# Loading the weights of the last two chunks in halves, to move the last store to another semaphore

## Chip, cores, metric

One core of a Trainium2 chip. PE is TensorE (matrix products), ACT is ScalarE, DVE is VectorE and POOL is GpSimd. The metric is the device time of one execution in microseconds (us). It lies 1.8 us above the span of the profile.

## The reference

```python
B, S, D, F = 32, 32, 1024, 3584          # all bf16
def reference(x, w_gate, w_up, w_down):
    return (gelu_tanh(x @ w_gate) * (x @ w_up)) @ w_down
```

1024 tokens, two matrices of 1024 x 3584 and one of 3584 x 1024. The kernel spends fewer multiplications than that by working with sums and differences of quadrants of the matrices; those sums are made on POOL (GpSimd) and wait for weights.

## The kernel before

The first stage goes through 14 chunks of weights; the second multiplies by `w_down`. Weights of a chunk are loaded two chunks ahead, by SyncE:

```python
    def load_w(eng, ci, which, d0, d1):
        f0 = ci * FC * P
        src = (wg_r, wu_r)[which]
        eng.dma_start(out=w_tiles[ci, which][:, d0:d1, :], in_=src[:, d0:d1, f0 : f0 + FC * P])

    def load_w_all(ci, which):
        alloc_w(ci, which)
        load_w(nc.sync, ci, which, 0, KD if which == 0 and is_ahead(ci) else DT)
```

At the end four tiles are cast from PSUM and stored, the last one by ACT:

```python
        for m in range(MT):
            r0 = NB + m * P
            o = late.tile([P, NB], bf16, name="o_sb", tag="o_sb", bufs=MT)
            (nc.vector.tensor_copy if m % 2 == 0 else nc.scalar.copy)(o, banka[m])
            nc.scalar.dma_start(out=of[r0 : r0 + P, :NB], in_=o)
```

The framework adds the semaphores (counters that one part of the chip raises and another waits for). In the built program DMAs take eight semaphores in turn, in program order; a DMA raises its semaphore by 16 as its parts land (the trace of the kernel before has 1472 such steps for 92 DMAs). At the end SyncE waits for all of them, two semaphores to a wait: first 3 and 2, then 4 and 1, then 5 and 0, then 6 and DVE's, then 7 and ACT's. Before the change the last store is on DMA semaphore 3, so the *first* of the five waits is the one that really waits.

## Time and profile before

275.1 us, median of three runs (274.97 to 275.95). The profiled run took 274.77 us.

The page of the kernel before (share of the span behind each engine; then the chain of work that ended last, as shares of the span):

```profile
span 273.0 us, 3360 instructions
## 1 busy us (share of the span) xinstructions
PE 268.6 (98%) x1206; PEld 188.7 (69%) x1206; DVE 195.3 (72%) x196; ACT 110.9 (41%) x181; POOL 108.1 (40%) x55
...
## 4 chain that ended last, share of the span: by engine, by line
PE 98%; ACT 0%; DVE 0%; issue 0%
```

PE is the limit from start to end. A change that is to gain anything must shorten PE's work or one of the two ends of the span, where PE is not busy all the time (27.56 of the first 28.50 us, and not at all after 269.51, the end of its last matmul). The windows of the kernel before (PE's busy time is the second number) show no idle PE in the middle:

```profile
core 0: us, PE busy (x) PEld busy (x) DVE busy (x) ACT busy (x) POOL busy (x), PEclk, DMA share, GB/s
0.00:28.50 28.50, 27.56 (x134) 13.17 (x134) 15.15 (x18) 9.75 (x12) 0.70 (x6) 1.00 0.85 212
...
100.00:180.00 80.00, 80.00 (x358) 56.86 (x357) 51.15 (x67) 42.76 (x78) 48.26 (x22) 1.00 0.29 83
180.00:260.00 80.00, 80.00 (x359) 57.23 (x358) 73.13 (x49) 19.39 (x20) 0.00 (x0) 1.00 0.56 181
```

The end, from the timeline of the kernel before (start, duration, engine, line, operation; in brackets what ended the idle time): the last cast, then the issue of the last store.

```profile
269.55 0.58 ACT L580 CAST o_sb<-psA 128x512 bf16<-128x512 f32 x1 [2.59 <-PE psA L440]
270.17 0.34 ACTq L581 DMA_DIRECT2D out_dram<-o_sb  x1
```

What follows is shown by the waits of the DMA queue's engine, SyncE (waiter, releaser, us in total, times, longest): one wait of 23.4 us for stores, and no second one.

```profile
SPq L605 <- DMA out_dram<-o_sb: 23.4, 1, 23.4
```

In the trace itself the last store lands at 271.89 and SyncE's end reads like this (start in us, operation, what it waits for; semaphores by their place among the eight):

```
271.910  wait  DMA 3 and DMA 2      <- the last store is on 3
271.979  wait  DMA 4 and DMA 1
272.041  wait  DMA 5 and DMA 0
272.105  wait  DMA 6 and DVE
272.167  wait  DMA 7 and ACT
272.232  drain, then two barriers of all engines, to 272.984
```

The first wait's record starts 0.02 us after the landing at 271.893, so a record's start is read here as the moment at which the wait is satisfied. The other four, whose last DMA had landed at 268.71, are walked through one by one, 62 to 69 ns from one to the next and 0.257 us from the first to the last. From the landing to the end of the span it is 1.09 us.

POOL's sum that waits for the last weights:

```profile
0.77 2.72 PE L229 MATMUL psA<-const-bfloat16-1.0 128*128 128x512 bf16 x6 [0.77 <-PEq L594]
3.29 0.63 PE L237 MATMUL tp<-ident,x_nat 128*128 128x128 bf16 x4
4.09 0.48 PE L279 MATMUL psC<-b,a12a 128*128 128x256 bf16 x2 [0.17 <-DVE b L240]
...
6.16 0.38 PE L246 MATMUL psA<-b,wg 128*128 128x512 bf16 x1
```

```profile
158.00 2.52 POOL L162 TENSOR_TENSOR s<-wu 128x1024 fp32r<-128x1024 bf16 x1 [4.02 <-DMA wu<-in_w_up_dram]
```

### The profile page before, as it was taken

What the parts mean: (1) busy time and instruction counts of PE and PEld (TensorE: products, weight loads), DVE (VectorE), ACT (ScalarE), POOL (GpSimd) and SP (SyncE); (2) the same over time, 40 slices, a digit from 0 to 9 for tenths busy, and PEclk for the clock granted to TensorE, in tenths of its full rate; (3) what the DMA queues carried; (4) which work ended last, traced back from release to release, by engine and by line L of the source; (5) the groups of instructions that cost most, each with busy time, mean ns of one, the idle gap of its engine ahead of it and who ended that gap; (6) DMA issues with size and microseconds to landing.
All of it is one profiled execution on the core that took longest, in us unless ns stands there. A gap on an engine that the chain in (4) does not pass through costs nothing.

```text
span 273.0 us, 3360 instructions
## 1 busy us (share of the span) xinstructions
PE 268.6 (98%) x1206; PEld 188.7 (69%) x1206; DVE 195.3 (72%) x196; ACT 110.9 (41%) x181; POOL 108.1 (40%) x55
## 2 busy tenths in 40 slices
PE   8999999999999999999999999999999999999994
PEld 4444777877877677676868686754447888888883
DVE  1269996887756676766757656459999999999611
ACT  1271665454543645555463636430300023962001
POOL 1000099997897794948577584000000000000000
PEclk9999999999999999999999999999999999999999
DMA  7994330423504505050513280005992446686202
GB/s 184 292 249 105 95 102 13 118 63 93 156 27 126 151 5 155 0 154 5 151 47 108 67 282 0 0 2 164 346 298 79 129 140 185 218 282 201 78 0 78
DMA packets 53777, 33.77 MB, mean 124 GB/s; under 512 B 9728, under 2 KB 53760, under 8 KB 53760
## 3 DMA queue, kind: packets, MB, share of 16 engines
q1 hardware_dynamic: 50240, 31.00, 39.3%
q10 hardware_dynamic: 3520, 2.56, 2.9%
q8 instruction: 9, 0.15, 0.2%
q14 instruction: 8, 0.07, 0.1%
HBM read 29.62 MB, written 2.10 MB: 116 GB/s over the span
## 4 chain that ended last, share of the span: by engine, by line
PE 98%; ACT 0%; DVE 0%; issue 0%
PE psA L264 34%; PE psA L440 18%; PE psC L264 17%; PE psC L440 7%; PE psB L440 7%; PE psB L264 5%; PE psB L246 3%; PE psA L246 3%; PE psC L279 2%; PE psA L279 1%; PE psA L229 1%; ACT o_sb L580 0%; PE tp L237 0%; DVE b L240 0%
## 5 line engine op out<-in xcount | busy, mean ns | idle before, releaser
L264 PE MATMUL psA<-t,s 128*128 128x512 f32 x208 | 54.1, 402 | 0.0
L256 ACT ACTIVATE h<-c 128x512 bf16<-128x512 f32 x52 | 31.6, 627 | 36.6 <-DVE c L344 36.6
L264 PEld LDWEIGHTS psA<-t,s 128*128 128x128 f32 x208 | 39.1, 188 | 9.2
L162 POOL TENSOR_TENSOR s<-wu 128x1024 fp32r<-128x1024 bf16 x12 | 27.5, 2294 | 24.4 <-PE psC L264 16.0
L344 DVE TENSOR_TENSOR c<-sn,psA 128x512 f32<-128x512 f32 x26 | 17.7, 683 | 16.7 <-PE psA L264 16.7
L264 PEld LDWEIGHTS <-wg 128*128 128x128 bf16 x168 | 15.4, 98 | 20.1 <-issue 3.4
L163 POOL TENSOR_TENSOR s<-s,wg 128x1024 fp32r<-128x1024 f32 x12 | 27.4, 2283 | 0.9
L165 POOL TENSOR_TENSOR s<-wg,wu 128x1024 fp32r<-128x1024 bf16 x12 | 26.6, 2215 | 0.0
L349 ACT COPY sn<-psA 128x512 f32<-128x512 f32 x42 | 23.6, 584 | 6.7 <-PE psA L264 6.7
L349 ACT COPY sn<-psC 128x512 f32<-128x512 f32 x26 | 15.2, 588 | 26.9 <-PE psC L264 22.7
L264 PE MATMUL psA<-t,a22r 128*128 128x512 f32 x104 | 25.9, 391 | 0.0
L264 PE MATMUL psC<-t,s 128*128 128x512 f32 x104 | 25.8, 390 | 0.0
L264 PE MATMUL psC<-b22r,s 128*128 128x512 f32 x104 | 25.7, 389 | 0.0
L264 PE MATMUL psA<-b,wg 128*128 128x512 bf16 x104 | 24.6, 380 | 0.0
L264 PEld LDWEIGHTS psC<-t,s 128*128 128x128 f32 x104 | 19.4, 188 | 4.4 <-ACT ahead L371 0.3
L264 PEld LDWEIGHTS psA<-t,a22r 128*128 128x128 f32 x104 | 19.5, 188 | 4.1
L264 PEld LDWEIGHTS psC<-b22r,s 128*128 128x128 f32 x104 | 19.5, 188 | 4.1
L344 DVE TENSOR_TENSOR c<-sn,psC 128x512 f32<-128x512 f32 x26 | 17.7, 687 | 5.5 <-PE psC L264 5.5
L363 DVE TENSOR_TENSOR hi<-h,psA 128x512 bf16<-128x512 bf16 x14 | 9.6, 688 | 13.9 <-PE psA L264 13.9
L419 DVE TENSOR_TENSOR lo<-c,h 128x512 bf16<-128x512 f32 x12 | 17.9, 1490 | 0.6
L164 POOL TENSOR_TENSOR s<-wg,s 128x1024 fp32r<-128x1024 bf16 x8 | 17.3, 2158 | 0.6
L483 ACT COPY snb<-psC 128x512 f32<-128x512 f32 x4 | 2.2, 590 | 36.5 <-PE psC L440 36.5
(94 smaller groups left out, 413.2 us busy)
## 6 DMA issues: line engine op xcount, KB each, us to landing
wu<-in_w_up_dram SPq DMA_DIRECT2D x13, 512.0 KB, 4.0
wdb<-in_w_down_dram SPq DMA_DIRECT2D x12, 512.0 KB, 5.4
wdb<-in_w_down_dram SPq DMA_DIRECT2D x12, 384.0 KB, 4.8
wg<-in_w_gate_dram SPq DMA_DIRECT2D x8, 512.0 KB, 5.2
v<-in_w_down_dram SPq DMA_DIRECT2D x4, 512.0 KB, 6.4
out_dram<-o_sb ACTq DMA_DIRECT2D x16, 128.0 KB, 1.7
wg<-in_w_gate_dram SPq DMA_DIRECT2D x6, 256.0 KB, 4.5
v<-in_w_down_dram SPq DMA_DIRECT2D x4, 384.0 KB, 8.0
```

Source lines behind the costliest of these rows:

```text
L162: yield eng.tensor_tensor(s1, a21, a22, ADD)
L163: yield eng.tensor_tensor(s2, s1, a11, SUB)
L164: yield eng.tensor_tensor(s4, a12, s2, SUB)
L165: yield eng.tensor_tensor(s3, a11, a21, SUB)
L246: nc.tensor.matmul(ps, lhsT=w_tiles[0, which][:, dt, fl * P : (fl + 1) * P], rhs=x_rows(dt, nb), start=(dt == first), stop=(dt == last),)
L256: nc.scalar.activation(h, src, ACT.Gelu_apprx_tanh)
L264: nc.tensor.matmul(ps, lhsT=lhs[:, k, :], rhs=rhs[:, k, :], start=(start and k == 0), stop=(k == KD - 1), skip_group_check=True,)
L344: tt(t, s, ps, ADD)
L349: nc.scalar.copy(t, ps)
L363: tt(g_of(ft)[:, :NB], h0, psa, MUL)
L419: tt(g_of(ft)[:, NB:], added(sn5[fl], psa[fl]), h1[fl], MUL)
L440: nc.tensor.matmul(banks[m], lhsT=lhs(k)[:, m * P : (m + 1) * P], rhs=rhs(k), start=(start and k == 0), stop=(k == HF - 1), skip_group_che ...
```

## The change

The weights of the last two chunks come in two loads each. That makes four DMAs more, so every later DMA moves on by four of the eight semaphores, and the last store falls on semaphore 7, which the last of the five waits names. The first four waits can then be passed before the last store has landed.

```diff
     def load_w_all(ci, which):
         alloc_w(ci, which)
-        load_w(nc.sync, ci, which, 0, KD if which == 0 and is_ahead(ci) else DT)
+        if ci < NCH - 2:
+            load_w(nc.sync, ci, which, 0, KD if which == 0 and is_ahead(ci) else DT)
+            return
+        for d0 in (0, KD):
+            load_w(nc.sync, ci, which, d0, d0 + KD)
```

## The prediction

> **What bounds the kernel now.** The page gives PE 98% of the span (268.6 of 273.0 us), and the chain that ended last is PE for 98% of it. By windows, PE is busy all 10.00 us of every 10 us from 120 to 260, at granted clock 1.00. DVE (72%), ACT (41%), POOL (40%) and DMA (39% on the main queue) hide behind it. In the timeline the last matmul ends at 269.5; then come the last cast (0.585 us), the last store's issue at 270.165, its landing at 271.89, and the end of the program.
>
> **The end of the program.** On SyncE five semaphore waits, each for two semaphores, start at 271.910, 271.979, 272.041, 272.105 and 272.167; then drains and barriers, to 273.0. The first names the semaphore of the last store. So it passes 0.02 us after the landing, and the four behind it, whose semaphores were long complete, are walked through afterwards at 62 to 69 ns each: 0.257 us. [...] The 1.72 us from the last store's issue to its landing is not touched.
>
> **What the change does.** The built program shows four more loads (two weight tensors of two chunks, each 512 KB now twice 256 KB); bytes and packets stay. DMA semaphores go round eight, so all later DMAs move on by four: the last store goes from the third semaphore to the seventh (counted from zero), which the fifth and last wait names. The waits keep their order. The store before lands at 270.38, so the first four waits will have passed by about 270.5, and only the fifth remains after the last landing. Removed from the chain: 0.257 us.
>
> **What it adds.** Four issues on SyncE (0.37 to 0.53 us each), one more wait instruction there and one on ACT, some waits on POOL and PE for the other halves. The first down-projection loads, from 153.9, start 0.4 to 0.8 us later; they had landed by 164.3 and are first used at 179.8. POOL waited 4.02 us for the last up weights and began at 158.00; they may land up to 0.5 us later, but that sum is ready at 160.5 and first used at 168.8: 8 us of slack. The other three loads have more. PE waits for two more loads, long complete by then; the chunk pitch is 12.56 us whichever waits a chunk has. The order of computing instructions is the same on every engine. On the chain: 0 to 0.05 us.
>
> **Prediction.** 275.1 - 0.26 = 274.85 us, 0.1% faster: 274.3 to 275.4 holds it 8 times in 10. The three runs of before spread over 1 us, four times the gain, so one comparison may show either sign. Faster by over 2%: 0.5%; within 2%: 99%; slower by over 2%: 0.5%.
>
> **What would show it.** After: one SyncE wait follows the last landing, not five; from last landing to end of span is 0.84 us where it was 1.10; PE still 268.6 us busy, pitch 12.56; POOL's last wait for up weights is 4.0 to 4.6 us. If PE busy or the pitch grew, the halves cost something; if the tail is shorter but the median is not, it drowned in the spread.
>
> **What would make it wrong.** The last store lands later in its new place; [...] halved loads disturb each other so that POOL's sums come late; or the median of before was off by itself.

The sum stands as 275.1 - 0.26 (the 0.257 us of four waits, from the trace of before) = 274.85 us.

## More of the kernel before

At the start PE is kept busy with a few matmuls on constants while the first loads come in (`NWARM` is 6):

```python
        warm_ps = acc("A")
        for _ in range(NWARM):
            nc.tensor.matmul(warm_ps, lhsT=ones_w, rhs=ones_m, start=True, stop=True)
```

## The result, and the profile after

275.26 us, median of six runs (274.75 to 275.64), against 275.11 for six of the kernel before (274.89 to 275.95). The ratio is 1.0, with a 95% interval of 0.9983 to 1.0016. (Such a ratio is the mean time of one kernel's fast runs over that of the other's of the same rounds, so not quite the ratio of the medians.) The time lies in the predicted range. But a gain of 0.26 us is a ratio of 0.9991: the interval holds that as well as none at all, and the medians even went the other way. The time alone does not say whether the mechanism worked.

The profile of after does. Its page:

```profile
span 273.3 us, 3350 instructions
## 1 busy us (share of the span) xinstructions
PE 267.9 (98%) x1190; PEld 188.9 (69%) x1206; DVE 196.6 (72%) x196; ACT 110.8 (41%) x181; POOL 108.3 (40%) x55
```

PE's busy time is lower only because 16 of its 1206 matmul records are missing in this trace; the busy time is not the thing to compare. The end, in timeline and SyncE's waits of after:

```profile
270.18 0.58 ACT L586 CAST o_sb<-psA 128x512 bf16<-128x512 f32 x1 [2.59 <-PE psA L446]
270.80 0.34 ACTq L587 DMA_DIRECT2D out_dram<-o_sb  x1
```

```profile
SPq L611 <- DMA out_dram<-o_sb: 23.7, 5, 11.3
```

The one wait of 23.4 us has become five with 23.7 us in total: each really waits now, for another store. In the trace, with the last landing at 272.506:

```
260.028  wait  DMA 3 and DMA 2
267.888  wait  DMA 4 and DMA 1
269.351  wait  DMA 5 and DMA 0
271.045  wait  DMA 6 and DVE
272.522  wait  DMA 7 and ACT       <- the last store is on 7
272.587  drain, then two barriers of all engines, to 273.343
```

Only one wait is left behind the landing, and from the landing to the end of the span it is 0.837 us instead of 1.091. The tail is shorter by 0.254 us; the prediction had 0.257.

So why is the span not shorter? Because all of it starts later. PE's first product of chunk 1, the first one of the regular part, starts at 28.578 before and at 29.178 after. From there to PE's last matmul it is 240.547 us before and 240.575 after. The whole difference of the two spans, 0.36 us, is +0.60 at the start, +0.03 in the regular part, -0.02 up to the last landing and -0.25 in the tail. The first 28 us, however, are before the first instruction that the change touches (a load issued at 129.4 us). The start of PE in the kernel after:

```profile
0.77 2.72 PE L235 MATMUL psA<-const-bfloat16-1.0 128*128 128x512 bf16 x6 [0.77 <-PEq L600]
3.29 0.63 PE L243 MATMUL tp<-ident,x_nat 128*128 128x128 bf16 x4
4.45 0.61 PE L285 MATMUL psC<-b,a12a 128*128 128x256 bf16 x2 [0.54 <-DMA a12a<-in_w_gate_dram]
4.86 0.53 PE L285 MATMUL psA<-b,a12a 128*128 128x256 bf16 x2
```

Two things differ from before. The first products start 0.37 us later, because a load that landed at 3.73 before landed at 4.41 now. And they run slower: two of them took 0.61 us, where it was 0.48. The records of PE's clock show why: the first one at full speed is at 5.15 us, before it was at 4.13. Either could be an accident of this one execution; what belongs to the change is the tail alone. That is a theory so far.

POOL's sum for the last chunk, which the halves might have delayed:

```profile
158.23 2.15 POOL L168 TENSOR_TENSOR s<-wu 128x1024 fp32r<-128x1024 bf16 x1 [3.75 <-PE psC L270]
```

It began 0.23 us later than before in a run that was 0.60 us late as a whole: the halves made it earlier, not later. Counted from the first issue, the last up weights had landed after 4.36 us as one load and after 3.94 us as two.

### The profile page after: what moved, and what is told of

The parts are those of the page before. It is cut to its first block, busy times and chain, and to the rows that moved or that the text cites. A ratio compares the mean times of both kernels' runs of the same rounds, so it can differ in the third digit from the quotient of the medians.

```text
span 273.3 us, 3350 instructions
## 1 busy us (share of the span) xinstructions
PE 267.9 (98%) x1190; PEld 188.9 (69%) x1206; DVE 196.6 (72%) x196; ACT 110.8 (41%) x181; POOL 108.3 (40%) x55
## 3 DMA queue, kind: packets, MB, share of 16 engines
q1 hardware_dynamic: 50304, 31.00, 39.3%
## 4 chain that ended last, share of the span: by engine, by line
PE 97%; DMA 1%; issue 0%; ACT 0%; SPq 0%
PE psA L270 34%; PE psA L446 18%; PE psC L270 17%; PE psC L446 7%; PE psB L446 7%; PE psB L270 5%; PE psB L252 3%; PE psA L252 2%; PE psC L285 2%; PE psA L285 1%; DMA a12a<-in_w_gate_dram 1%; ACT o_sb L586 0%; SPq L191 0%; PE tp L243 0%
## 5 line engine op out<-in xcount | busy, mean ns | idle before, releaser
L168 POOL TENSOR_TENSOR s<-wu 128x1024 fp32r<-128x1024 bf16 x12 | 27.4, 2285 | 23.7 <-PE psC L270 12.8
L425 DVE TENSOR_TENSOR hi<-c,h 128x512 bf16<-128x512 f32 x14 | 18.0, 1284 | 0.5
```

What stands on the lines that cost most here:

```text
L168: yield eng.tensor_tensor(s1, a21, a22, ADD)
L425: tt(g_of(ft)[:, NB:], added(sn5[fl], psa[fl]), h1[fl], MUL)
```

## The experiments

Three questions: Does the tail shorten the time, or do the halves cost on the way what the tail saves? Does the gain come from the place of the last store's semaphore, and in steps of one wait? And what makes the runs of one kernel differ by 1 us, four times the gain? In the table at the end of this section all profiles are decomposed.

The theories, as the expectations name them. A: the tail saves 0.26 us, the halves cost nothing, and the spread is in when the first loads land. B: the halves cost what the tail saves. C: the spread is the moment at which PE gets its full clock. D: it is in the loads or elsewhere.

### First batch: longer warm-up; the halves alone; the shift alone

`quiet_before` and `quiet_after` are the two kernels with

```diff
-    NWARM = 6
+    NWARM = 24
```

> The kernel before with 24 warm-up matmuls in place of 6, so that PE comes to its first real work some 4 to 8 us after the first loads landed and should no longer wait for them. Theory A (the change saves 0.26 us in the tail, but run-to-run spread in when the first loads land hides it): the time rises to about 279 to 283 us, and its runs spread far less than the 1 us of before, under 0.3 us. Theory B (the halves cost on the way what the tail saves; the spread comes from all over the program): the spread stays near 0.7 to 1 us. Both: from last landing to end of span 1.10 us.

> The changed kernel with the same 24 warm-up matmuls. Theory A: 0.2 to 0.3 us faster than quiet_before, clear of a small spread; from last landing to end of span 0.83 us; PE from the first product of chunk 1 to its last matmul within 0.05 us of quiet_before. Theory B: same time as quiet_before within 0.1 us, that stretch of PE 0.2 to 0.3 us longer.

Measured: quiet_before 279.79 us (279.24 to 280.24, four runs), quiet_after 279.16 us (278.80 to 279.81, four runs). The spread did not shrink: it is 1.0 us in both. PE no longer waits for loads here, so theory A is wrong about the spread. The start of PE in quiet_before and in quiet_after shows what it is instead:

```profile
0.77 8.03 PE L229 MATMUL psA<-const-bfloat16-1.0 128*128 128x512 bf16 x24 [0.77 <-PEq L594]
8.64 0.38 PE L237 MATMUL tp<-ident,x_nat 128*128 128x128 bf16 x4
```

```profile
0.77 7.12 PE L235 MATMUL psA<-const-bfloat16-1.0 128*128 128x512 bf16 x24 [0.77 <-PEq L600]
7.73 0.38 PE L243 MATMUL tp<-ident,x_nat 128*128 128x128 bf16 x4
```

The same 24 matmuls, which wait for nothing, took 8.03 us in one run and 7.12 in the other. Single ones start every 0.43 us at first and every 0.22 us later. The clock's first record at full speed is at 6.18 us in quiet_before and at 4.32 us in quiet_after: 1.86 us of half speed more, half of which is lost, 0.93 us; the first product of chunk 1 comes 0.91 us later. What sets the moment of the full clock, no run here shows. Over the 13 profiles it comes 2.94 us (tiny4, below) to 5.92 us (gated_after) after the first matmul, which is at 0.77 us.

The regular part of PE is 240.58 us in one and 240.55 in the other, the tail 1.092 and 0.845 us. The 0.63 us between the medians is more than the tail can give (0.25 us); with four runs each that spread over 1 us it is not to be read as the gain.

`halves8` has the last four chunks in halves: eight loads more, once round the semaphores, so that the last store is back on semaphore 3.

```diff
-        if ci < NCH - 2:
+        if ci < NCH - 4:
```

> Halves for the weights of the last four chunks, eight more loads: the semaphores go round once, and the last store is back on the semaphore that the end waits for first. Twice the suspected cost, no gain. Theory A: the tail is 1.10 us again with four waits behind the landing; PE's stretch from chunk 1 to the last matmul stays at 240.4 us; time that of before. Theory B: that stretch grows by 0.4 to 0.6 us over before, and the time with it.

Measured: 275.58 us (275.01 to 275.94, six runs), ratio to before 1.0 (0.9983 to 1.0018). The regular part of PE is 240.551 us: twice the halves cost nothing there. The tail is 1.092 us. Theory B is out by this trace; by the time alone it could not be said.

`tiny4` is the kernel before with four small loads that nobody uses:

```diff
         load_w(nc.sync, ci, which, 0, KD if which == 0 and is_ahead(ci) else DT)
+        if ci >= NCH - 2:
+            t = gpool.tile([P, P], bf16, name="spare", tag=f"spare{ci}{which}", bufs=1)
+            nc.sync.dma_start(out=t, in_=xf[:P, :P])
```

> The kernel before with four 32 KB loads into a tile that nobody reads, at the places of the halves: the shift of semaphores without the halves. Theory A: tail 0.83 us, PE's stretch 240.4 us, time like that of the change (within spread of 0.26 us under before). Theory B: tail 0.83 us and no cost of halves: clearly 0.26 us faster than the change, 274.85 or less.

Measured: 275.14 us (274.96 to 275.90, six runs), ratio 0.9993 (0.9974 to 1.0012): nothing to be read from the time. In the trace one wait is left behind the landing, as it should be, but the tail is 1.031 us and not 0.84. The rest went to the last barrier, where ACT came late: its drain started 0.37 us after the barrier before it, where it was 0.09 us in the other profiles of this batch, and the other engines waited. A miss of the expectation, taken up below.

### Second batch: a fixed start

If the spread is the clock, then a start that does not depend on the clock must remove it. PE gets 12 warm-up matmuls, and then one that waits for a short chain on POOL, which ended at 6.0 us whatever PE's clock did (the matmul behind it starts at 6.04 us in gated_before, gated_halves8 and gated_after, with the full clock at 5.17, 4.66 and 6.69 us):

```diff
-    NWARM = 6
+    NWARM = 12
...
             nc.tensor.matmul(warm_ps, lhsT=ones_w, rhs=ones_m, start=True, stop=True)
+        gate = xpool.tile([P, 1024], bf16, name="gate")
+        nc.gpsimd.memset(gate, 1.0)
+        for _ in range(2):
+            nc.gpsimd.tensor_tensor(gate, gate, gate, MUL)
+        nc.tensor.matmul(warm_ps, lhsT=gate[:, :P], rhs=ones_m, start=True, stop=True)
```

This costs time (some 2.4 us); it is an instrument and not an improvement. It was put on the four kernels before, after, halves8 and tiny4. They were run on another chip.

> The kernel before with a fixed start: 12 warm-up matmuls, then one that waits for a short chain on POOL of fixed length (three operations, ending at some 7 us), by when the clock record of every run so far shows full speed (first full-speed record at 3.7 to 6.2 us). Theory C (the spread of 1 us is the moment at which PE gets its full clock): the first product of chunk 1 starts within 0.1 us of the same place in each gated kernel, and the runs spread under 0.4 us; time 277 to 279 us. Theory D (the spread is in when the first loads land, or elsewhere): spread stays near 1 us.

> The changed kernel with the same fixed start. If the tail saves 0.25 us and the halves cost nothing: 0.2 to 0.3 us faster than gated_before, with the two sets of runs nearly apart under theory C; under theory D the sets overlap and the medians may fall either way. Tail from last landing to end 0.84 us against 1.09.

> Last four chunks in halves with the same fixed start: twice the halves, the last store back on the semaphore waited for first. If halves cost nothing: same as gated_before within 0.1 us, tail 1.09 us. If each four halves cost 0.25 us: 0.5 us slower than gated_before.

> Four tiny loads in place of the halves, same fixed start: the shift alone. As gated_after within 0.1 us, 0.2 to 0.3 us under gated_before. The tail was 1.03 us in the profile of tiny4, because ACT came 0.25 us late to the last barrier; if that belongs to this program and not to that one run, it comes again and the gain is only 0.06 us.

Measured, six runs each, on one chip, in the same rounds:

```
gated_before   277.62 277.61 277.85 277.62 277.66 277.86   median 277.64
gated_halves8  277.68 277.64 277.65 277.65 277.65 277.65   median 277.65
gated_tiny4    277.52 277.55 277.78 277.54 277.54 277.79   median 277.54
gated_after    277.63 277.34 277.35 277.43 277.32 277.36   median 277.35
```

The kernel before without the gate, run beside them, ranged from 274.81 to 277.04 us in eleven runs. The gate made that 0.25 to 0.31 us where there are two levels and 0.04 where there is one, and most runs of a level agree within 0.05, as theory C expects. The gate alone does not decide between C and D: at 6.0 us the loads that PE's first products wait for (landed at 3.73 and 4.41 us in the first two profiles) are in as well, so the gate takes out both. That the clock alone can make 0.91 us is shown by the quiet kernels; how much of the 2.2 us beside the gated runs was loads is open, because none of those runs was profiled.

The gate came sooner than expected (6.0 us, not some 7), too soon for one of the four profiles, which missed the expected 0.1 us: the profiled run of gated_after is its slowest one, 277.63 us, and in it the clock was at full speed only at 6.69 us, after the gate, where the other three profiles have 4.66 to 5.17 us. PE's start in gated_before and gated_after:

```profile
0.77 4.91 PE L229 MATMUL psA<-const-bfloat16-1.0 128*128 128x512 bf16 x12 [0.77 <-PEq L599]
6.04 0.39 PE L234 MATMUL psA<-const-bfloat16-1.0,gate 128*128 128x512 bf16 x1 [0.36 <-POOL gate L233]
6.27 0.39 PE L242 MATMUL tp<-ident,x_nat 128*128 128x128 bf16 x4
6.92 0.47 PE L284 MATMUL psC<-b,a12a 128*128 128x256 bf16 x2 [0.27 <-DVE b L245]
```

```profile
0.77 5.28 PE L235 MATMUL psA<-const-bfloat16-1.0 128*128 128x512 bf16 x12 [0.77 <-PEq L605]
6.04 0.61 PE L240 MATMUL psA<-const-bfloat16-1.0,gate 128*128 128x512 bf16 x1
6.44 0.51 PE L248 MATMUL tp<-ident,x_nat 128*128 128x128 bf16 x4
7.22 0.47 PE L290 MATMUL psC<-b,a12a 128*128 128x256 bf16 x2 [0.27 <-DVE b L251]
```

Both reach the gate at 6.04, but in the second the matmul behind it still runs at half clock (0.61 against 0.39 us), and the first product comes 0.30 us later. That is the step between the lower and the upper times of gated_after; that the upper times of gated_before and gated_tiny4 have the same cause is likely, but none of those runs was profiled.

With the start held still, the change is visible in the plain time. gated_after is 0.29 us below gated_before by the medians and 0.30 by the means (277.405 against 277.703). Without the runs at the upper level (two of gated_before, one of gated_after) the medians are 277.62 and 277.35, 0.27 us apart. gated_halves8 has twice the halves and its store on semaphore 3, and equals gated_before within 0.01 us by the medians (0.03 us above its lower level): **the halves cost nothing and gain nothing; the gain is the place of the last store's semaphore.**

Not all of this gain is the tail. The store's own way from issue to landing, which the prediction called untouched, is 1.73 to 1.76 us in the five profiles with the last store on semaphore 3 and 1.705 to 1.711 us in the six with it on 7 (table below). These 0.02 us or more come with the place of the store as well; why, no run shows.

And gated_tiny4, with that same place, gains only 0.10 us. Its profile has ACT late in the last barrier again (tail 1.025 us), so that belongs to this program.

### Third batch: step by step; ACT's late instruction

`gated_plus1` and `gated_plus2` put fewer weights in halves, so that the last store is on semaphore 4 (second wait) or 5 (third wait). The two edits in one:

```diff
-        if ci < NCH - 2:
+        if (ci, which) != (NCH - 1, 1):     # gated_plus1: one load more
+        if ci < NCH - 1:                    # gated_plus2: two loads more
```

> Fixed start, only the last of the four weights in halves: one more DMA, the last store on the semaphore of the second of the five waits, so three waits are left after the last landing. If each wait behind the landing costs 0.064 us: tail 1.03 us, time 277.58 us, 0.06 under gated_before (277.64). If the gain came from anything but the place of the wait, the time is that of gated_before or of gated_after (277.35).

> Fixed start, both weights of the last chunk in halves: two more DMAs, the last store named by the third of five waits, two left behind it. Tail 0.96 to 0.97 us, time about 277.50 us.

Measured: gated_plus1 277.55 us (277.53 to 277.56, five runs), tail 1.037 us. gated_plus2: the four runs are 277.48, 277.70, 277.69 and 277.48, two at each of two levels, 0.2 us apart as in gated_before, so the median of 277.59 falls between them; the lower level is 277.48, and the profile, which is of a run at that level, has a tail of 0.963 us. Counted as waits behind the landing:

```
waits behind the landing   kernel          tail us        time us, lower level
4                          gated_before    1.091          277.62
3                          gated_plus1     1.037          277.55
2                          gated_plus2     0.963          277.48
0                          gated_after     0.850          277.35
```

About 0.05 to 0.07 us for each wait, in tail and time alike. The third batch ran on another chip than the second (the kernel before took 275.37 and 275.28 us beside them), but the steps stand within the third batch too: gated_tiny4_pad, below, has no wait behind the landing and takes 277.35 us there.

`gated_tiny4_pad` is gated_tiny4 with one small instruction more on ACT, well before the end:

```diff
         for b in range(NBT):
             nc.scalar.copy(a22r[b], A22[b])
+        nc.scalar.copy(s5[0][:, :1], s5[0][:, :1])
```

> gated_tiny4 (277.54) with one more instruction on ACT, a one-column copy in the second stage. In gated_tiny4 and tiny4 ACT's 320th record was its second drain of the end and came 0.25 us late; in the changed kernel the 320th was the first drain, late by 0.33 us inside the wait for the last landing, where it costs nothing. If it is the place in the instruction stream: the late record is now the barrier wait before it, hidden, the tail is 0.84 us and the time that of gated_after, 277.35. If the lateness belongs to the tiny loads: it stays at 277.54.

Measured: 277.35 us (277.32 to 277.36, five runs), tail 0.845 us, which is gated_after to 0.01 us. It ran on another chip than gated_tiny4, but the two tails in the traces differ by the same 0.18 us. This is also the cleanest pair with gated_before, without any halves: in the two profiles the start is the same, the regular part is the same within 0.004 us, and of the 0.262 us between the spans 0.246 are the tail and 0.020 the store's way to its landing. So it is not the tiny loads that cost 0.19 us but where ACT's instructions stand. In tiny4 and gated_tiny4 the 320th instruction that the trace has for ACT is the drain of the last barrier and comes late. In after and halves8 ACT has two more (323 instead of 321), the 320th is the drain before it, and it is that one which comes late: in after at 271.467, 0.33 us after the issue before it had ended, in the middle of the wait for the last landing, where it costs nothing. One instruction more in gated_tiny4_pad, and the last barrier is on time. In all eight profiles in which the 320th is a drain it starts 0.32 to 0.37 us after the end of the instruction before it; in the other five it is a wait for the other engines, where lateness cannot be seen.

What makes it late, no run shows. One thing falls near it in the traces. The page lists two DMA queues of the kind "instruction"; for the kernel before:

```profile
q8 instruction: 9, 0.15, 0.2%
q14 instruction: 8, 0.07, 0.1%
```

In every profile a packet of 8 KB on queue 14 starts within 0.4 us after the start of ACT's 64th record and of its 192nd, and 0.64 to 0.72 us after its 320th in the eight profiles where that is a drain. So the place of the late instruction, 128 records after the 192nd, is one near which such a packet starts. But it starts only after the late instruction has started, so it is not what this one waited for, and no run moves such a packet alone.

### All profiles

Full clock is the first full-speed record; the regular part is from the first product of chunk 1 to the last matmul; the tail is from the last landing to the end of the span. All in us.

```
kernel            full    first product  regular   last issue   tail
                  clock   of chunk 1     part      to landing
before            4.13    28.578         240.547   1.728        1.091
after             5.15    29.178         240.575   1.711        0.837
halves8           6.10    29.435         240.551   1.761        1.092
tiny4             3.71    28.976         240.549   1.710        1.031
quiet_before      6.18    33.775         240.579   1.740        1.092
quiet_after       4.32    32.864         240.550   1.710        0.845
gated_before      5.17    31.399         240.576   1.727        1.091
gated_after       6.69    31.701         240.549   1.705        0.850
gated_halves8     4.66    31.407         240.575   1.752        1.086
gated_tiny4       4.93    31.404         240.549   1.710        1.025
gated_plus1       4.76    31.405         240.576   1.721        1.037
gated_plus2       5.20    31.406         240.575   1.706        0.963
gated_tiny4_pad   4.33    31.399         240.580   1.707        0.845
```

The regular part is one of two values, 240.55 or 240.58, in kernels with halves and without, so 0.03 us of a single comparison is of no kernel. Without a gate the first product lies between 28.58 and 29.44. The clock is not all of that: tiny4 had its clock first of all and was still 0.40 us behind before, having waited for the first weight load (its first product started at 4.46 us, that of before at 4.09). So load landings and clock both move the start; the quiet kernels show the clock alone.

No version beats both kernels by more than the change itself does: the gate costs 2.4 us, and the padded tiny loads only equal the change.

## Why the prediction was right or wrong

- What bounds the kernel (PE), that nothing on the chain is added, and a time within 2%: right.
- The tail: 0.257 us predicted, 0.254 us in the trace, 0.27 to 0.29 us in the time with a fixed start. The mechanism and its size were right; the 0.02 us beyond it is the store's way to its landing, which the prediction called untouched (1.727 us in gated_before, 1.707 in gated_tiny4_pad); the steps of gated_plus1 and gated_plus2 show that it goes wait by wait. "the first four waits will have passed by about 270.5": the fourth passed 0.015 us after the landing of the store before the last (271.03, in a run that was 0.63 us late), as meant.
- The halves: no cost. gated_halves8 shows it in the time (0.01 us), halves8 in the regular part. "The first down-projection loads [...] start 0.4 to 0.8 us later": 0.55 us, counted from the issue of the up weights ahead of them (0.42 us before, 0.97 after). "they may land up to 0.5 us later", of POOL's last up weights: wrong in sign and without effect; in halves they landed 0.43 us sooner after their issue. "bytes and packets stay": the packets of the main queue went from 50240 to 50304, sixteen for each load more, without effect.
- The predicted median of 274.85 was not met: 275.26, in the range, and 0.15 us above before instead of 0.26 below. The prediction said that one comparison may show either sign, and why that is so was left open ("the median of before was off by itself"). It is the start: the moment of the full clock, which differed from 3.71 to 6.18 us between ungated profiles, and the landing of the first loads (3.73 us before, 4.41 after). The place of the median in the range was therefore luck of the runs. The prediction had the spread as a number and not its cause.
- "PE still 268.6 us busy" was a bad sign to watch: 267.9, because of missing records. The length of a stretch from one matmul to another was the good one.
- What the runs show is a late instruction (0.32 to 0.37 us), of a cause not shown: in tiny4 it came at the wrong place and took 0.19 us of the gain. In the changed kernel the late one fell, by chance, into a wait.

## What to carry to other kernels

At the end of the programs here the waits for semaphores are walked through in a fixed order, and every one that stood behind the last landing cost 0.05 to 0.07 us; let the last store be on the semaphore that is waited for last, by whatever shifts the count cheaply, and look at the tail in the trace afterwards: the tiny loads shifted it too and lost 0.19 us of the gain to ACT. A gain of a thousandth cannot be seen in times that spread four times as much: cut the span in the trace into start, regular part and tail, and if the time itself has to show it, hold the start still with a gate, on both kernels alike. And compare with twice the suspected cost at no gain (the halves of four chunks): that told more than repeating the pair.
